# Batch 0's q and k loaded in two parts, w_out ahead of batch 1's v, the last subtile in two column halves: one change to the opening and the tail of an attention + MLP kernel

## The chip, the cores and the metric

One core of a Trainium2 chip. The time is the device time of one execution in microseconds (us). A kernel is run several times beside the kernel before on the same chip, and its median is quoted with the lowest and highest run. A run counts as "slow" when it lies over 1.5% above the fastest of its kernel.

## The reference

Eight batches of causal attention with a decay bias, then a two-layer MLP over all 4608 tokens, in fp32:

```python
scores = scale * q @ k.T                     # 8 batches, 8 heads, 576 tokens, 64 wide
cum    = cumsum(maximum(s, 0))
scores = where(causal, -1e9, scores + minimum(-(cum_i - cum_j), 0))
x      = softmax(scores) @ v                 # -> (4608, 512)
out    = gelu(x @ w_in) @ w_out              # w_in 512 x 2048, w_out 2048 x 512
```

## The kernel before

The tensor engine is kept busy from end to end: the MLP of one chunk of 512 tokens runs with the attention of the next batch woven between its matmuls ("side lists"). Only the opening, where everything waits for loads, and the tail are thin. All loads of q, k, v and the weights are issued by gpsimd. `filler(n)` is n matmuls on zeros: they do no work, they fill a wait. Some words used below: a subtile is 128 tokens. An attend is the product of the softmax weights with v, for which VectorE or gpsimd first scales v (the tile `vv`). PSUM is the memory, divided into banks, that takes the tensor engine's results.

The loads of batch 0's q and k, one per tensor and head group, are 128 runs of 18 tokens (4.5 KB) each, back to back in memory, into 128 partitions:

```python
def qk_runs(src, b, g0, n):                  # LT = 18 tokens per partition
    return bass.AP(tensor=src.tensor, offset=src.offset + (b * H + 4 * g0) * S * D,
                   ap=[[LT * D, 128], [4 * S * D, n], [1, LT * D]])
for g in range(HG):
    for i in range(2):                       # q, k
        load_qk(0, i, g, 1)
```

The opening (cut):

```python
filler(17); cum_sum(); masks(); weights()
nc.scalar.activation(vv[0][:, :, :, D], wb[:, :, 0:H], func=AF.Copy)
filler(3)
filler(3, raws[0, "qk"][:, 1, 0, :128])      # waits for the first k
load_v(0, nc.gpsimd, (0, 1)); load_w(0, 0); load_w(0, 1)       # load_w(0, i): quarter i of w_in
load_v(0, nc.gpsimd, (2, 3)); load_w(0, 2); load_w(0, 3)
scale_v(0, 1, nc.gpsimd)
load_v(0, nc.gpsimd, (4,)); load_qks(1)
load_w(1, 0); load_w(1, 1); load_v(1, nc.gpsimd, (0, 1))       # load_w(1, i): quarter i of w_out
load_w(1, 2); load_w(1, 3); load_v(1, nc.gpsimd, (2, 3, 4))
tr_qk(0, 0, 0); tr_qk(0, 1, 0); sc_first(0, 0)                 # transposes, first scores
# ... the remaining scores, masks, attends and transposes of batch 0
```

The tail. The kernel computes on its way whether its shortcuts hold for the data; a flag is then loaded into a register of each engine, and a branch goes around the general path:

```python
# last subtile: 16 matmuls of 128x512 into one PSUM tile
rv = nc.values_load(bad[0:1, 0:1], min_val=0, max_val=1)
with tc.If(rv > 0):
    ...                                      # general path (not taken here)
y = y_of[LAST[0], sub]
for i, (copy, eng) in enumerate([(nc.vector.tensor_copy, nc.sync), (scalar_copy, nc.scalar)]):
    cols = slice(i * 256, i * 256 + 256)
    copy(o_sb, y[:, cols]); eng.dma_start(out=out[r0 : r0 + 128, cols], in_=o_sb)
```

## Time and profile before

| | kernel before |
|---|---|
| time, median of 3 runs | 315.48 us (315.06 to 315.62) |
| first score / first layer / second layer of chunk 0 starts | 10.23 / 19.46 / 36.74 us |
| first layer of chunk 1 starts | 56.48 us |
| mean granted clock of the tensor engine | 0.999 |

The rows of the table come from the tensor engine's work in order of time, in one profiled run; that run took 315.94 us, 0.4 above the median. The prediction below shows the main lines of the profile. From the page, the clock granted to the tensor engine in 40 slices of 7.85 us (9 is 90% or more) and the count of DMA packets:

```profile
PEclk9999999999999999999999999999999999999999
DMA packets 30979, 36.46 MB, mean 116 GB/s; under 512 B 15648, under 2 KB 20000, under 8 KB 30944
```

And the last matmuls in the timeline (start, duration, what): they end at 305.78 + 3.19 = 308.97, 0.51 us before the first copy at 309.48.

```profile
305.78 3.19 PE L483 MATMUL o_ps<-w_out_r,gT 128*128 128x512 bf16 x14
```

### The profile page before, as it was taken

The numbers are of one execution on the slowest core, as the hardware profiler recorded it, in microseconds if no ns is written. First come the engines' busy times: TensorE is split into PE (matmuls) and PEld (weight loads), VectorE is DVE, ScalarE is ACT, GpSimd is POOL, SyncE is SP. The second block draws the span as 40 slices with busy tenths as digits, with TensorE's granted clock in tenths as the row PEclk, the third lists the DMA queues.
The fourth block names the chain that finished last, engine by engine and source line by source line (L and its number), as shares of the span: only waits on it lengthen the run. The fifth ranks groups of instructions, "written<-read, shape, count | busy, mean of one in ns | idle before, by whom it ended". The sixth has DMA issues, their size and how long they took to land. (4 is left out here: it accounts for less than half of the span.)

```text
span 314.2 us, 6059 instructions
## 1 busy us (share of the span) xinstructions
PE 302.0 (96%) x2475; PEld 155.5 (49%) x2516; DVE 199.0 (63%) x398; ACT 191.0 (61%) x258; POOL 54.5 (17%) x73
## 2 busy tenths in 40 slices
PE   8899999999999999999999999999999999999993
PEld 3477755544554455545454455444544555444441
DVE  7776658599769856975598459955895532250020
ACT  2786878887737673875586658756776666105400
POOL 8653341133001500070007000500000000000000
PEclk9999999999999999999999999999999999999999
DMA  7999999779521973179307951633101331010012
GB/s 124 222 230 209 225 211 270 163 140 211 141 84 25 199 173 102 22 166 206 102 17 171 190 118 36 143 79 91 50 19 42 102 52 26 33 72 32 1 68 75
DMA packets 30979, 36.46 MB, mean 116 GB/s; under 512 B 15648, under 2 KB 20000, under 8 KB 30944
## 3 DMA queue, kind: packets, MB, share of 16 engines
q0 software_dynamic: 11552, 23.07, 38.1%
q1 hardware_dynamic: 19248, 12.80, 14.4%
q8 instruction: 21, 0.34, 0.4%
q14 instruction: 14, 0.11, 0.1%
q10 hardware_dynamic: 144, 0.13, 0.1%
HBM read 36.85 MB, written 9.44 MB: 147 GB/s over the span
## 5 line engine op out<-in xcount | busy, mean ns | idle before, releaser
L483 PE MATMUL o_ps<-w_out_r,gT 128*128 128x512 bf16 x551 | 132.2, 379 | 2.4 <-issue 1.6
L467 PE MATMUL h_ps<-xT,w_in_r 128*128 128x512 bf16 (+1 forms) x625 | 131.4, 357 | 1.3 <-DVE xT L413 0.5
L472 ACT ACTIVATE gT<-h_ps 128x1024 bf16<-128x1024 f32 (+1 forms) x80 | 75.1, 939 | 64.5 <-PE h_ps L467 63.7
L467 PEld LDWEIGHTS <-w_in_r 128*128 128x128 bf16 x640 | 59.8, 98 | 54.2 <-issue 0.6
L483 PEld LDWEIGHTS <-gT 128*128 128x128 bf16 x576 | 51.9, 98 | 56.6 <-issue 3.0
L359 ACT ACTIVATE P<-sc_ps 128x1024 bf16<-128x1024 f32 x56 | 54.3, 1021 | 30.5 <-PE sc_ps L344 30.5
L122 POOL DMA_DIRECT2D raw_v<-in_v_dram x40 | 34.1, 863 | 128.4 <-ACT sq L213 115.7
L493 DVE COPY o_sb<-o_ps 128x512 f32<-128x512 f32 x31 | 21.4, 691 | 46.5 <-PE o_ps L483 46.5
L444 DVE RECIPROCAL rc<-av 128x4 f32<-128x4 f32 (+1 forms) x80 | 14.0, 175 | 39.4 <-PE av L435 39.3
L187 DVE STREAM_TRANSPOSE qkT<-raw_qk 128x576 f32<-128x576 f32 x32 | 37.4, 1242 | 1.8 <-DMA raw_qk<-in_k_dram 1.7
L445 DVE TENSOR_TENSOR x<-av,rc 128x256 bf16<-128x256 f32 (+1 forms) x80 | 33.8, 423 | 3.0
L435 PEld LDWEIGHTS <-P 128*128 128x128 bf16 x576 | 27.1, 97 | 16.5 <-issue 0.8
L205 DVE TENSOR_REDUCE amx<-raw_qk 128x2 f32<-128x2304 bf16 x14 | 35.1, 2532 | 0.0
L435 PE MATMUL av<-vv,P 128*128 128x65 bf16 x576 | 30.5, 193 | 0.6 <-POOL vv L221 0.2
L367 DVE TENSOR_TENSOR P<-P,tri_bf 128x1024 bf16<-128x1024 bf16 (+1 forms) x33 | 22.0, 669 | 9.1 <-ACT P L359 9.1
L221 DVE TENSOR_TENSOR vv<-raw_v,wb 128x512 bf16<-128x512 f32 (+1 forms) x39 | 25.4, 690 | 2.5 <-DMA raw_v<-in_v_dram 2.5
L213 ACT ACTIVATE sq<-raw_v 128x512 bf16<-128x512 f32 (+1 forms) x40 | 24.8, 621 | 0.0
L344 PE MATMUL sc_ps<-qkT 32*128 32x256 bf16 (+2 forms) x560 | 18.2, 250 | 0.0
L344 PEld LDWEIGHTS <-qkT 32*128 32x128 bf16 x560 | 11.7, 92 | 12.4 <-issue 11.6
L498 ACT ACT_TABLE_LOAD x8 | 10.3, 1283 | 0.9 <-PEq L817 0.8
L419 PE MATMUL f_ps<-zero 128*128 128x512 bf16 x26 | 9.3, 494 | 1.2 <-DVE zero L150 1.2
L501 ACT ACT_TABLE_LOAD x8 | 10.3, 1283 | 0.1
(81 smaller groups left out, 92.3 us busy)
## 6 DMA issues: line engine op xcount, KB each, us to landing
out_dram<-o_sb SPq DMA_DIRECT2D x35, 256.0 KB, 2.2
raw_v<-in_v_dram POOLq DMA_DIRECT2D x32, 256.0 KB, 5.5
raw_qk<-in_q_dram POOLq DMA_DIRECT2D x7, 576.0 KB, 7.5
raw_qk<-in_k_dram POOLq DMA_DIRECT2D x7, 576.0 KB, 10.4
w_in_r<-in_moe_w_in_dram POOLq DMA_DIRECT2D x4, 512.0 KB, 12.1
w_out_r<-in_moe_w_out_dram POOLq DMA_DIRECT2D x4, 512.0 KB, 15.8
raw_v<-in_v_dram POOLq DMA_DIRECT2D x8, 128.0 KB, 6.4
raw_qk<-in_q_dram POOLq DMA_DIRECT2D x2, 288.0 KB, 6.2
```

Of the source, the lines that this page charges most:

```text
L122: eng.dma_start(out=t[:n_st, st, :, :], in_=bass.AP(tensor=v.tensor, offset=v.offset + b * H * S * D + st * 128 * D, ap=[[D, n_st], [S * D ...
L187: nc.vector.transpose(qkT[b % 2][:, i, g, :S, :].rearrange("p s e -> p (s e)").bitcast(fp32) .rearrange("p (l j) -> p j l", j=LT), raws[b, ...
L205: nc.vector.tensor_reduce(amx[:, b * HG + g], raws[b, "qk"][:, :, g, :], axis=AX, op=ALU.max, apply_absolute_value=True,)
L213: nc.scalar.activation(sq[:n_st], raws[b, "v"][:n_st, st].rearrange("p h d -> p (h d)"), func=AF.Square, accum_out=sumv[:n_st, b, st : st ...
L221: eng.tensor_tensor(vv[b % 2][:n_st, st, :, 0:D], raws[b, "v"][:n_st, st, :, :], w.unsqueeze(2).to_broadcast([n_st, H, D]), op=MULT,)
L344: nc.tensor.matmul(s_ps[h // 2][:, h % 2, off : off + n], lhsT=qk[r, 1, g, jt * 128 : jt * 128 + 128, e], rhs=qk[r, 0, g, i0 : i0 + n, e], ...
L359: nc.scalar.activation(P[:, 2 * h2 : 2 * h2 + 2, o : o + 512], s_ps[h2], func=AF.Exp, scale=scale)
L435: nc.tensor.matmul(o_ps[:, h, :], lhsT=P[:, h, off : off + 128], rhs=vv[b % 2][:, jt, 4 * g + h, :], start=(i == 0), stop=(i == len(BLK[it ...
L445: nc.vector.tensor_tensor(x_of[b, it][:n, g * 256 : g * 256 + 256].rearrange("p (h d) -> p h d", d=D), o_ps[:n, :, 0:D], rc[:n].unsqueeze( ...
L467: nc.tensor.matmul(h_ps[:, i, :], lhsT=w_in_r[:, ko, ft * 128 : (ft + 1) * 128], rhs=xT[:, ko, c * NB + n0 : c * NB + n1], start=(ko == 0) ...
L472: nc.scalar.activation(gT_of[c][:, f2 * 2 : f2 * 2 + 2, n0:n1], h_ps, func=AF.Gelu)
L483: nc.tensor.matmul(y_of[c, sub], lhsT=gT[:, ft, sub * 128 : (sub + 1) * 128], rhs=w_out_r[:, ft, :], start=(ft == 0), stop=(ft == FT - 1),)
```

## The change

Three things. (1) The opening: q and k of batch 0 come in two parts, tokens 0 to 383 of all heads first, so that scores can start earlier; the order of the opening's work and of gpsimd's loads follows. (2) All of w_out is issued ahead of batch 1's v, and the scalings of v move to later groups of the side lists. (3) The last subtile is computed as two column halves in two PSUM banks, so that the two last copies need not follow one another.

```diff
+    PART = [(0, 384), (384, 576)]
+    def load_part(i, g, part):
+        t0, t1 = PART[part]
+        n = (t1 - t0) // 32 * D
+        src = q if i == 0 else k
+        nc.gpsimd.dma_start(
+            out=raw_qk(0)[:, i, g, t0 * 2 : t1 * 2],
+            in_=bass.AP(tensor=src.tensor, offset=src.offset + 4 * g * S * D + t0 * D,
+                        ap=[[S * D, 4], [n, 32], [1, n]]))
...
-            load_qk(0, i, g, 1)
+            load_part(i, g, 0)
... # after weights():
-    nc.scalar.activation(vv[0][:, :, :, D], wb[:, :, 0:H], func=AF.Copy)
-    filler(3)
-    filler(3, raws[0, "qk"][:, 1, 0, :128])
+    for g in range(HG):
+        for i in range(2):
+            load_part(i, g, 1)
+    filler(1)
+    filler(2, raws[0, "qk"][:, 1, 0, :128])
... # issue order: v0 v1 w0 w1 v2 w2 v3 w3 v4, then
-    load_w(1, 0); load_w(1, 1); load_v(1, (0, 1)); load_w(1, 2); load_w(1, 3); load_v(1, (2, 3, 4))
+    load_w(1, 0..3); load_v(1)
... # batch 1's side lists
-  side[0] = [(sc, b, 0, 0), (scale_v, b, 0), (scale_v, b, 1), (mk, b, 0, 0)]
-  side[5] = [(sc, b, 0, 1), (av, b, 0, 0), (av, b, 0, 1)]
-  side[6] = [(av, b, 1, 0, True), (av, b, 1, 1, True), (scale_v, b, 2), (mk, b, 0, 1)]
-  ...
+  side[0] = [(sc, b, 0, 0), (mk, b, 0, 0)]
+  side[5] = [(sc, b, 0, 1)]
+  side[6] = [(scale_v, b, 0), (scale_v, b, 1), (av, b, 0, 0), (av, b, 0, 1), (mk, b, 0, 1)]
+  side[7] = [(sc, b, 1, 1), (av, b, 1, 0, True), (av, b, 1, 1, True), (gelu_set,)]
+  side[8] = [(scale_v, b, 2), (to_xT, b, 0, True), (av, b, 0, 2), (mk, b, 1, 1)]
+  side[9] = [(to_xT, b, 1, True), (scale_v, b, 3), (av, b, 0, 3)]
... # last subtile
+        for cols in (slice(0, 256), slice(256, 512)):
+            y = yps.tile([128, KO * 128], fp32, tag="mlp", bufs=2, name="o_ps")[:, :256]
+            for ft in range(FT):
+                nc.tensor.matmul(y, lhsT=gT_of[c][:, ft, ...], rhs=w_out_r[:, ft, cols], ...)
```

More of the change, by code (lines that the diff above doesn't have):

```diff
@@ L108, in load_qk, with tr_part @@
         )
+    PART = [(0, 384), (384, 576)]
[5 more added lines that the diff above has]
+            out=raw_qk(0)[:, i, g, t0 * 2 : t1 * 2],
+            in_=bass.AP(
+                tensor=src.tensor, offset=src.offset + 4 * g * S * D + t0 * D,
+                ap=[[S * D, 4], [n, 32], [1, n]],
+            ),
+        )
+    def tr_part(i, g, part):
+        t0, t1 = PART[part]
+        n = (t1 - t0) // 32
+        nc.vector.transpose(
+            qkT[0][:, i, g, t0:t1, :].rearrange("p s e -> p (s e)").bitcast(fp32)
+            .rearrange("p (l j) -> p j l", j=n),
+            raws[0, "qk"][:, i, g, t0 * 2 : t1 * 2].bitcast(fp32).rearrange("p (j w) -> p j w", j=n),
+        )
     def load_qks(b):
@@ L474, in l1_item, with l2_last, l2_item @@
         )
-    def l2_item(c, subs, f0=0, f1=FT, store=True):
+    def l2_last(c, sub):
+        y_of[c, sub] = []
+        for cols in (slice(0, 256), slice(256, 512)):
+            y = yps.tile([128, KO * 128], fp32, tag="mlp", bufs=2, name="o_ps")[:, :256]
+            y_of[c, sub].append((cols, y))
+            for ft in range(FT):
+                nc.tensor.matmul(
+                    y, lhsT=gT_of[c][:, ft, sub * 128 : (sub + 1) * 128], rhs=w_out_r[:, ft, cols],
+                    start=(ft == 0), stop=(ft == FT - 1),
+                )
+    def l2_item(c, subs, f0=0, f1=FT):
         gT = gT_of[c]
@@ L486, in l2_item @@
                 )
-        if f1 == FT and store:
+        if f1 == FT:
             for sub in subs:
@@ L516 @@
     weights()
-    nc.scalar.activation(vv[0][:, :, :, D], wb[:, :, 0:H], func=AF.Copy)
-    filler(3)
-    filler(3, raws[0, "qk"][:, 1, 0, :128])
+    for g in range(HG):
[3 more added lines that the diff above has]
+    filler(2, raws[0, "qk"][:, 1, 0, :128])
     load_v(0, nc.gpsimd, (0, 1))
+    nc.gpsimd.tensor_copy(vv[0][:, :, :, D], wb[:, :, 0:H])
     load_w(0, 0)
     load_w(0, 1)
-    load_v(0, nc.gpsimd, (2, 3))
+    load_v(0, nc.gpsimd, (2,))
+    scale_v(0, 1, nc.gpsimd)
     load_w(0, 2)
+    load_v(0, nc.gpsimd, (3,))
     load_w(0, 3)
-    scale_v(0, 1, nc.gpsimd)
     load_v(0, nc.gpsimd, (4,))
     load_qks(1)
-    load_w(1, 0)
-    load_w(1, 1)
-    load_v(1, nc.gpsimd, (0, 1))
-    load_w(1, 2)
-    load_w(1, 3)
-    load_v(1, nc.gpsimd, (2, 3, 4))
-    tr_qk(0, 0, 0)
-    tr_qk(0, 1, 0)
+    for i in range(4):
+        load_w(1, i)
+    load_v(1, nc.gpsimd)
+    for g in range(HG):
+        for i in range(2):
+            tr_part(i, g, 0)
     sc_first(0, 0)
-    tr_qk(0, 0, 1)
-    tr_qk(0, 1, 1)
-    sc_first(0, 1, (0,))
-    filler(1)
     sc_first(1, 0, (0,))
+    tr_part(0, 0, 1)
+    tr_part(1, 0, 1)
     mk_item(0, 0, 0)
     scale_v(0, 0)
+    filler(1)
     sc_first(1, 0, (1,), 0)
+    filler(1)
+    sc_first(0, 1, (0,), 0)
+    mk_item(0, 1, 0, 0, 2)
     av_item(0, 0, 0)
+    mk_item(0, 1, 0, 2, 4)
+    tr_part(0, 1, 1)
+    tr_part(1, 1, 1)
     av_item(0, 0, 1)
-    mk_item(0, 1, 0, 0, 2)
-    sc_first(0, 1, (1,))
-    mk_item(0, 1, 0, 2, 4)
-    sc_first(1, 1, (0,), 0)
+    sc_first(0, 1, (1,), 0)
     av_item(0, 1, 0)
     av_item(0, 1, 1)
+    sc_first(1, 1, (0,), 0)
+    to_xT(0, 0, True)
     sc_first(1, 1, (1,), 0)
-    to_xT(0, 0, True)
-    filler(1)
     to_xT(0, 1, True)
@@ L621 @@
                 side = [[] for _ in range(16)]
-                side[0] = [(sc, b, 0, 0), (scale_v, b, 0), (scale_v, b, 1), (mk, b, 0, 0)]
+                side[0] = [(sc, b, 0, 0), (mk, b, 0, 0)]
                 side[3] = [(sc, b, 1, 0), (mk, b, 1, 0)]
-                side[5] = [(sc, b, 0, 1), (av, b, 0, 0), (av, b, 0, 1)]
-                side[6] = [(av, b, 1, 0, True), (av, b, 1, 1, True), (scale_v, b, 2), (mk, b, 0, 1)]
-                side[7] = [(to_xT, b, 0, True), (sc, b, 1, 1)]
-                side[8] = [(to_xT, b, 1, True), (scale_v, b, 3), (av, b, 0, 2), (gelu_set,), (mk, b, 1, 1)]
-                side[9] = [(av, b, 0, 3)]
+                side[5] = [(sc, b, 0, 1)]
[3 more added lines that the diff above has]
+                side[9] = [(to_xT, b, 1, True), (scale_v, b, 3), (av, b, 0, 3)]
                 side[11] = [(av, b, 1, 2, True), (scale_v, b, 4), (square_qk, 0, 0), (square_qk, 0, 1)]
@@ L657 @@
             for sub in range(4):
-                l2_item(c, (sub,), store=(c, sub) < LAST)
+                if (c, sub) < LAST:
+                    l2_item(c, (sub,))
+                else:
+                    l2_last(c, sub)
                 if c == B - 1:
@@ L768, in layer_1, with layer_2 @@
                     nc.scalar.activation(g[:, ft, :n], h_ps[:, :n], func=AF.Gelu)
-            def layer_2(h_ps, g, sub):
+            def layer_2(h_ps, g, sub, cols=slice(0, 512)):
                 for ft in range(FT):
                     nc.tensor.matmul(
-                        h_ps, lhsT=g[:, ft, sub * 128 : (sub + 1) * 128], rhs=w_out_r[:, ft, :],
+                        h_ps, lhsT=g[:, ft, sub * 128 : (sub + 1) * 128], rhs=w_out_r[:, ft, cols],
                         start=(ft == 0), stop=(ft == FT - 1),
@@ L789 @@
             for sub in range(LAST[1], 4):
-                layer_2(y_of[LAST[0], sub], g, sub)
+                for cols, y in y_of[LAST[0], sub]:
+                    layer_2(y, g, sub, cols)
     with tc.manual_schedule():
         for sub in range(LAST[1], 4):
-            y = y_of[LAST[0], sub]
             r0 = LAST[0] * NB + sub * 128
-            for i, (copy, eng) in enumerate(
-                [(nc.vector.tensor_copy, nc.sync), (lambda o, a: nc.scalar.activation(o, a, func=AF.Copy), nc.scalar)]
+            for (cols, y), copy, eng in zip(
+                y_of[LAST[0], sub],
+                (nc.vector.tensor_copy, lambda o, a: nc.scalar.activation(o, a, func=AF.Copy)),
+                (nc.sync, nc.scalar),
             ):
-                cols = slice(i * 256, i * 256 + 256)
                 o_sb = ost.tile([128, KO * 128], fp32, tag="osb", bufs=3, name="o_sb")[:, :256]
-                copy(o_sb, y[:, cols])
+                copy(o_sb, y)
                 eng.dma_start(out=out[r0 : r0 + 128, cols], in_=o_sb)
```

## The prediction

> **What bounds the kernel now.** I read the page first (busy shares, slices, DMA row), then what the tensor engine waits for, then its work in order of time for the first 60 us, then the gpsimd engine's in the same stretch (it issues all loads), then each tile's landing times, last the tail.
>
> The page:
> ```profile
> PE 302.0 (96%) x2475; PEld 155.5 (49%) x2516; DVE 199.0 (63%) x398; ACT 191.0 (61%) x258; POOL 54.5 (17%) x73
> DMA  7999999779521973179307951633101331010012
> ```
> The tensor engine is busy from end to end, and nothing in the change removes matmuls that matter, so only the opening and the tail can move. The DMA row (7.85 us a slice) is full through slice 7 and nearly so to slice 10: loads are dense for some 60 us.
>
> The tensor engine's work in time (start us, duration, then what it is):
> ```profile
> 10.23 0.63 PE L389 MATMUL sc_ps<-qkT 32*128 32x256 bf16 x8 [0.47 <-DVE qkT L187]
> ...
> 15.21 0.37 PE L435 MATMUL av<-vv,P 128*128 128x65 bf16 x7 [0.24 <-POOL vv L221]
> 15.51 0.63 PE L389 MATMUL sc_ps<-qkT 32*128 32x256 bf16 x12
> ...
> 19.46 3.65 PE L467 MATMUL h_ps<-xT,w_in_r 128*128 128x256 bf16 x32 [0.52 <-DVE xT L413]
> ...
> 25.88 1.04 PE L467 MATMUL h_ps<-xT,w_in_r 128*128 128x256 bf16 x8
> ...
> 44.57 1.03 PE L483 MATMUL o_ps<-w_out_r,gT 128*128 128x512 bf16 x4
> ```
> First scores at 10.23, first layer at 19.46. At 15.21 the engine waited for a product that gpsimd made. The loads as gpsimd issues them, and the landing times of the two weight tiles (min/median/max):
> ```profile
> 12.14 0.75 POOL L147 DMA_DIRECT2D w_in_r<-in_moe_w_in_dram  x1 [0.77 <-DMA raw_qk<-in_k_dram]
> 14.05 1.10 POOL L221 TENSOR_TENSOR vv<-raw_v,wb 128x512 bf16<-128x512 f32 x1 [1.17 <-DMA raw_v<-in_v_dram]
> ...
> 26.11 1.55 POOL L147 DMA_DIRECT2D w_out_r<-in_moe_w_out_dram  x2 [1.95 <-DMA w_in_r<-in_moe_w_in_dram]
> ```
> ```profile
> DMA to landing us min/median/max: 9.9/12.1/13.7
> ```
> ```profile
> DMA to landing us min/median/max: 14.9/15.8/17.5
> ```
> The last quarter of w_in lands at 12.14 + 13.7 = 25.84, and its first user runs at 25.88. The last quarter of w_out is issued at about 26.88 and lands at 44.4 (+17.5); its first user runs at 44.57. No wait is listed at either place, yet both matmuls follow the landing at once: **the opening is tuned to arrive with its weights.** So I take 25.84 and 44.4 as floors, not coincidences. This is the reading on which the number rests.
>
> The tail:
> ```profile
> 309.48 0.42 DVE L801 COPY o_sb<-o_ps 128x256 f32<-128x256 f32 x1 [3.23 <-DVEq L664]
> 309.94 0.38 ACT L797 ACTIVATE o_sb<-o_ps 128x256 f32<-128x256 f32 x1 [13.72 <-DVE o_sb L801]
> 310.35 0.37 ACTq L802 DMA_DIRECT2D out_dram<-o_sb  x1
> ```
> Two half copies, one after the other: ScalarE waits for VectorE's, as both read one PSUM tile.
>
> **What the Trainium skill says.** "PSUM — Partial Sum Buffer", section "PSUM bank collisions raise a hardware error": two engines may not access one bank in the same partitions at once, readers included, so software orders them. The trace agrees: 309.48 + 0.42, then 309.94. "TensorE: Matmul & The Clock Gate", Part 1: a warm matmul costs N / 2.4 GHz + 2.5 ns from start to start, 109 ns for N = 256 and 216 for 512. The trace agrees: 32 of N = 256 take 3.65 us, less some 0.17 of drain, 109 ns each. "DMA: Bandwidth & Descriptors", section "Why a DMA increments its semaphore by 16 and not by 1": the number of DMA engines k is the largest up to 16 that divides the slowest dimension of both sides, with some gpsimd copies as exceptions. Before, q and k have 128 runs on both sides. The parts have 4 (heads) x 32 at the source, so k may be 4. No load of the trace before has that form, so this stays open.
>
> **The change, part by part.**
>
> *Scores earlier.* The four batch-0 loads were issued at 1.25 to 3.01 and landed, issue plus landing time, at 5.95, 8.9, 10.3 and 11.85. A first part is 2/3 of one. Read off that progress, the four first parts land at about 4.9, 6.9, 8.9 and 9.9; if each runs on 4 engines they go side by side and land at about 7.3, 8.0, 8.5 and 9.1. A transpose of 576 tokens takes 1.24 us, so 384 take about 0.85. The second transpose, which the first score needs, ends near 8 to 9.1. Scores start 1.1 to 2.0 us earlier than 10.23, ScalarE's first exp likewise earlier than 10.90. The transposes become eight instead of four but have the same elements; perhaps 0.2 us more of VectorE, hidden.
>
> *What becomes of that lead.* The second attend item of head group 0 needs vv of subtile 1, which gpsimd makes after v's subtile 1 has landed: 14.05 + 1.10 = 15.15. The same bytes (all q, k, then two subtiles of v) lie ahead of it after the change, so it still comes at about 15.15, and the next score stands behind it on the tensor engine in both kernels. The lead of 1 to 2 us therefore ends at 15.2. What is left is the reordering after it. From 15.5: score 0.57, attend 0.5, score 0.57, transpose 0.25, then the last score, which waits for the sixth exp, near 17.3, then transpose and the 0.42 copy: the first layer starts near 18.9, 0.6 ahead of 19.46. One filler (0.22) and one wait on VectorE are gone from this stretch.
>
> *w_in.* The order is now w0, w1, v2, w2, v3, w3 instead of w0, w1, v2, v3, w2, w3. w2 lands 1 us earlier (22.0 for 23.0), which the earlier start needs. The bytes ahead of w3 do not change, so it lands at 25.8 again. The first layer, 0.6 ahead, gets at most 0.45 ahead at that place (work alone puts it at 25.4) and nothing if w3 comes at 25.84. I expect 0.05 to 0.2 there.
>
> *w_out ahead of v.* It takes 0.52 MB of v, two loads that took about 1.05 us each, from ahead of w2 and w3 of w_out: they land near 39 and 42, no longer a limit. Now v's first two subtiles land last, at the same 44.4. VectorE's scaling takes 0.69 more, so the second attend of group 6 can start at about 45.15. In the tensor engine's time it would come at 45.05 + 0.11 less any lead. So the lead is clipped again: work done by 45.43 before is done by about 45.4 after. The floor moves from one tensor to another; the bytes do not change.
>
> *gpsimd.* A copy of 40 columns moves there from ScalarE (0.38 us there) and waits for the weights (8.5). With eight part loads the first v load waits for the first part to land, and w0 is issued near 9.2 to 10 instead of 6.2, w2 near 15.1 instead of 10.6. The DMA row shows the engines full throughout; bytes outstanding still cover about 2 us, so I expect no hole, but this margin is thin.
>
> *Tail.* 16 matmuls of 512 (15 x 215 + 379 ns = 3.61 us) become 32 of 256 (31 x 109 + 273 = 3.65): +0.04. The two copies then lie in two banks and start together: the later store goes out at about 309.95 instead of 310.35, -0.40. Both copies still wait for the branch around the general path, so the first half cannot be copied under the second. Net -0.36.
>
> **Sum.** -0.36 at the tail, -0.1 to -0.2 at w3, about 0 at 44.4 beyond that, and about -0.15 as an allowance for a DMA stream that gains from part loads side by side. Together -0.65: 315.48 becomes **314.8**.
>
> **Rivals.**
> 1. *The lead survives.* Should the landings at 25.84 and 44.4 be coincidence, or should the stream run faster from the start (between 4 and 6 us it writes at 146 GB/s, later 200 to 270), the lead of 0.6 would stay, more if v's subtile 1 comes earlier too. Total 313.6 to 314.3. For it: no wait for a weight is on the tensor engine's list. Against it: two floors met within 0.2 us.
> 2. *The loads get slower.* Four engines a load, starting one after the other, leave a quarter of them idle until 4 us; runs are shorter, there are four more loads, gpsimd issues later. A shift of w3 passes to the end undiminished: with 1 us, 315.8. Against it: the first loads are slow already, so engine time is not what is short.
> 3. *A stall at batch 1's attend.* v's subtile 1 or its scaling comes 0.5 to 1 us late in group 6. Total 315.3 to 315.8. The dense DMA row speaks for it; against it, w_out leaves the queue earlier by the same amount.
> 4. *A gain over 2%* would need 6.3 us. The tensor engine idles less than that in the whole opening, so I give it nearly nothing.
>
> **Range and chances.** The tail is nearly certain (-0.3 to -0.45). The opening is -1.4 to +0.7, as w3 goes. Eight in ten: 313.8 to 315.7. Faster by over 2%: 0.02; within: 0.97; slower: 0.01.
>
> **What would show each step.** The list of issues: landing times of the parts (side by side means k = 4). Work in time: first score near 8.5 to 9.2; the attend still released by gpsimd's product near 15.15; first layer near 18.9; the w3 matmuls at 25.4 to 25.9, with a wait on the weight tile now or no gain; the attends after group 6 at 44.9 to 45.4, released by VectorE's scaling. Chain of waits: the two last copies together, about 0.4 us less behind them. I am wrong if the first-layer matmuls on w3 start a full microsecond earlier or later than 25.88, or if the attend of 15.2 moves with the scores.

## More of the kernel before

An engine's sequencer is the part that issues its instructions and takes its branches.

The granted clock is the share of full speed that the profile says the tensor engine was given.

## The result, and the profile after

| | before | after |
|---|---|---|
| median (lowest to highest), 4 runs each | 315.55 us (315.06 to 315.70) | 328.69 us (328.16 to 329.02) |
| ratio of fast runs, 95% interval | | 1.0418 (1.0400 to 1.0436) |
| first score starts | 10.23 | 12.11 |
| first layer of chunk 0 starts | 19.46 | 25.38 |
| second layer of chunk 0 starts | 36.74 | 45.17 |
| first layer of chunk 1 starts | 56.48 | 67.06 |
| from last matmul's end to first copy | 0.51 | 2.47 |

A ratio here and below compares the fast runs of the two kernels, so it is not quite the ratio of the medians that are quoted. The change is 4.2% slower; the predicted range ended at 315.7.

The table gives the shape: 8.43 us are lost before the second layer of chunk 0 starts (45.17 - 36.74), 2.15 more by the next chunk's first layer (67.06 - 56.48 = 10.58), and about 2 at the tail.

**Opening, loads.** What the DMA queues did in the first 4 us. In order, before and then after: packets of all queues, then those of the queue that serves gpsimd's loads with the MB they moved and the share of the 16 DMA engines' time that they took, then the loads issued with the median time from issue to landing.

```profile
DMA packets 174, 0.36 MB, mean 91 GB/s; under 512 B 16, under 2 KB 16, under 8 KB 174
q0 software_dynamic: 94, 0.22, 35.9%
raw_qk<-in_k_dram POOLq DMA_DIRECT2D x2, 288.0 KB, 7.9
```
```profile
DMA packets 749, 0.17 MB, mean 42 GB/s; under 512 B 674, under 2 KB 685, under 8 KB 749
q0 software_dynamic: 669, 0.02, 15.6%
raw_qk<-in_k_dram POOLq DMA_DIRECT2D x2, 192.0 KB, 9.4
```

A part has two thirds of the bytes and takes longer to land: 9.4 us for 7.9. In these 4 us the queue handled seven times the packets and moved a tenth of the bytes: nearly all of its packets are tiny (4 bytes each by the trace's packet records). But they do not fill the engines: its packets took 15.6% of the engines' time where they took 35.9% before, and from 4 to 8 us 72.9% for 99.0%. The whole execution shows the tiny packets too. From the page after:

```profile
PEclk9856999999999999999999999999999999999998
DMA packets 34627, 36.48 MB, mean 111 GB/s; under 512 B 18784, under 2 KB 24160, under 8 KB 34592
```

There are 18784 - 15648 = 3136 more packets under 512 B. Four more loads than before are 64 of them: 16 come with each load (the queue of gpsimd's loads has 1056 in the kernel before, for 66 loads). The other 3072 are 3 for each of the 8 x 128 = 1024 runs of the part loads.

**Opening, clock.** The other new thing in this page is the clock row: slices 2 to 4 stand at 8, 5 and 6, where before all stood at 9. By stretches (length, then busy time of the tensor engine, its weight loads, VectorE, ScalarE and gpsimd, granted clock, DMA share, GB/s), before and then after:

```profile
14.00:20.00 6.00, 4.99 (x84) 3.78 (x84) 4.64 (x15) 5.61 (x6) 4.00 (x5) 1.00 1.18 231
20.00:30.00 10.00, 9.70 (x127) 8.67 (x124) 6.68 (x21) 7.50 (x16) 4.90 (x6) 1.00 1.17 212
```
```profile
14.00:20.00 6.00, 6.00 (x52) 3.02 (x53) 3.39 (x9) 3.79 (x4) 3.22 (x5) 0.50 1.17 202
20.00:30.00 10.00, 8.98 (x74) 6.32 (x71) 5.90 (x16) 5.55 (x6) 6.45 (x10) 0.50 1.21 233
```

From 14 to 30 us the tensor engine ran at half clock: "6.00 of 6.00 busy" is 52 matmuls for the 84 of before (not all of the same shapes). The reader who looks only at busy shares would take the after kernel's stretch for the better one. The tensor engine's work in order of time, after, shows what came just ahead:

```profile
11.22 0.61 PE L443 MATMUL f_ps<-zero,raw_qk 128*128 128x512 bf16 x2 [2.74 <-DMA raw_qk<-in_k_dram]
12.11 0.63 PE L413 MATMUL sc_ps<-qkT 32*128 32x256 bf16 x8 [0.28 <-DVE qkT L128]
...
14.10 1.03 PE L413 MATMUL sc_ps<-qkT 32*128 32x256 bf16 x8
...
53.98 0.37 PE L459 MATMUL av<-vv,P 128*128 128x65 bf16 x7 [0.17 <-DVE vv L245]
...
57.90 0.37 PE L459 MATMUL av<-vv,P 128*128 128x65 bf16 x7 [0.39 <-DVE vv L245]
...
60.74 0.37 PE L459 MATMUL av<-vv,P 128*128 128x65 bf16 x7 [1.35 <-DVE vv L245]
```

The first line: the engine stood 2.74 us for the first part of k. Its next score of eight matmuls takes 0.63 us, and the one at 14.10 takes 1.03: the clock fell between them.

**Second layer of chunk 0.** The last three lines above: the attend waits three times for VectorE's scaled v (1.91 us in all). No such waits are listed there before.

**Tail.** The last 32 narrow matmuls, and the copies:

```profile
315.95 3.66 PE L507 MATMUL o_ps<-w_out_r,gT 128*128 128x256 bf16 x32
316.15 0.69 DVE L529 COPY o_sb<-o_ps 128x512 f32<-128x512 f32 x1 [2.76 <-PE o_ps L519]
322.08 0.38 ACT L841 ACTIVATE o_sb<-o_ps 128x256 f32<-128x256 f32 x1 [15.27 <-PEq L707]
322.08 0.42 DVE L845 COPY o_sb<-o_ps 128x256 f32<-128x256 f32 x1 [5.24 <-PEq L707]
```

The copies do start together, as intended, but both are released by the tensor engine's sequencer (PEq) at the line of the branch: 322.08 - (315.95 + 3.66) = 2.47 us after the last matmul ended.

So there are three candidate causes in the opening (slow loads, the fallen clock, the new order), one in the middle and one at the tail. The experiments take them one at a time.

### The profile page after: what moved, and what is told of

The parts are those of the page before. It is cut to its first block, busy times and chain, and to the rows that moved or that the text cites. A ratio compares the mean times of both kernels' runs of the same rounds, so it can differ in the third digit from the quotient of the medians.

```text
span 327.2 us, 6093 instructions
## 1 busy us (share of the span) xinstructions
PE 308.5 (94%) x2487; PEld 160.0 (49%) x2527; DVE 198.7 (61%) x402; ACT 190.9 (58%) x257; POOL 58.5 (18%) x78
## 2 busy tenths in 40 slices
DMA packets 34627, 36.48 MB, mean 111 GB/s; under 512 B 18784, under 2 KB 24160, under 8 KB 34592
## 5 line engine op out<-in xcount | busy, mean ns | idle before, releaser
L491 PE MATMUL h_ps<-xT,w_in_r 128*128 128x512 bf16 (+1 forms) x624 | 134.0, 363 | 1.4 <-DVE xT L437 0.5
L519 PE MATMUL o_ps<-w_out_r,gT 128*128 128x512 bf16 x536 | 129.2, 379 | 2.2 <-issue 1.4
L491 PEld LDWEIGHTS <-w_in_r 128*128 128x128 bf16 x640 | 61.1, 100 | 55.5 <-issue 0.7
L519 PEld LDWEIGHTS <-gT 128*128 128x128 bf16 x560 | 50.3, 98 | 54.7 <-issue 3.0
L383 ACT ACTIVATE P<-sc_ps 128x1024 bf16<-128x1024 f32 x56 | 54.3, 1021 | 30.5 <-PE sc_ps L368 30.5
L459 PE MATMUL av<-vv,P 128*128 128x65 bf16 x576 | 31.4, 195 | 2.8 <-DVE vv L245 2.1
L211 DVE STREAM_TRANSPOSE qkT<-raw_qk 128x576 f32<-128x576 f32 x28 | 32.4, 1239 | 0.0
L421 ACT ACTIVATE P<-sc_ps 128x1024 bf16<-128x1024 f32 x8 | 8.1, 1022 | 8.6 <-PE sc_ps L413 8.6
```

The costliest lines, as they stand in the source:

```text
L211: nc.vector.transpose(qkT[b % 2][:, i, g, :S, :].rearrange("p s e -> p (s e)").bitcast(fp32) .rearrange("p (l j) -> p j l", j=LT), raws[b, ...
L383: nc.scalar.activation(P[:, 2 * h2 : 2 * h2 + 2, o : o + 512], s_ps[h2], func=AF.Exp, scale=scale)
L459: nc.tensor.matmul(o_ps[:, h, :], lhsT=P[:, h, off : off + 128], rhs=vv[b % 2][:, jt, 4 * g + h, :], start=(i == 0), stop=(i == len(BLK[it ...
L491: nc.tensor.matmul(h_ps[:, i, :], lhsT=w_in_r[:, ko, ft * 128 : (ft + 1) * 128], rhs=xT[:, ko, c * NB + n0 : c * NB + n1], start=(ko == 0) ...
L519: nc.tensor.matmul(y_of[c, sub], lhsT=gT[:, ft, sub * 128 : (sub + 1) * 128], rhs=w_out_r[:, ft, :], start=(ft == 0), stop=(ft == FT - 1),)
```

## The experiments

Twelve kernels, all correct against the reference by the comparison used. Some read wrong tokens of batch 0's q and k, which is said where it holds; the comparison passes all the same, so it is no check on these tokens.

### 1. parts_flat: the part loads in another form

The changed kernel, with each part load reading 128 runs of the same length back to back (wrong tokens).

```diff
-    offset=src.offset + 4 * g * S * D + t0 * D,     ap=[[S * D, 4], [n, 32], [1, n]],
+    offset=src.offset + 4 * g * S * D + 4 * t0 * D, ap=[[n, 128], [1, n]],
```

> The changed kernel with its eight part loads of q and k reading 128 evenly spaced runs instead of 4 heads x 32 runs: same number of loads, same run lengths, same bytes, wrong tokens (the result is wrong on purpose). Theory A, the form of the source pattern (its slowest dimension is 4) makes the loads slow and sprinkles them with tiny packets: packets under 512 B fall by about 3070 (three for each of the 1024 runs), the last quarter of w_in lands near 25.8 us instead of 29.6, the clock stays at 1.0, and the time is 318.5 to 320.5 (what is left over before is the stall in the first second-layer pass, about 2.15, and the tail, about 2.35). Rival B, shorter runs and more loads are what is slow: as the changed kernel, 327 to 329.

Measured: 322.29 us (321.61 to 323.59), ratio 1.0223 (1.0188 to 1.0258). From its page:

```profile
PEclk9959999999999999999999999999999999999997
DMA packets 31555, 36.47 MB, mean 114 GB/s; under 512 B 15712, under 2 KB 21088, under 8 KB 31520
```

The 3072 tiny packets are gone (18784 - 15712), with the same number of loads and runs. The parts of k land 5.8 us after issue for 9.4, the queue's share of the engines' time in the first 4 us is 34.9% for 15.6%, and the first score starts at 8.43 instead of 12.11. Theory A holds on the form of the load: 6.4 us come back. The time is some 2 us above its range. A part of that is the clock, which falls here too, later and for a shorter time (number 5 gets 1.0 us back by holding it):

```profile
13.54 0.33 PE L459 MATMUL av<-vv,P 128*128 128x65 bf16 x5 [0.47 <-DVE vv L245]
14.91 0.37 PE L459 MATMUL av<-vv,P 128*128 128x65 bf16 x7 [1.04 <-POOL vv L245]
...
16.47 0.62 PE L459 MATMUL av<-vv,P 128*128 128x65 bf16 x8 [0.39 <-DVE x L469]
17.03 1.03 PE L413 MATMUL sc_ps<-qkT 32*128 32x256 bf16 x12
```

The engine, now early, waits for v in small pieces: 1.90 us in all. By the trace's clock records the clock falls at 16.03, after the first two of these waits (0.47 and 1.04) and at the start of the third; at 16.47 eight attend matmuls take 0.62 instead of 0.41.

### 2. before_4x32: the form alone, put into the kernel before

The kernel before, with whole loads whose source has the form heads x 32 runs. Each run starts 17 tokens after the last instead of 18, so that the two dimensions do not merge into one of 128 (wrong tokens, same sizes and number of loads).

```diff
-            load_qk(0, i, g, 1)                     # ap=[[LT * D, 128], ..., [1, LT * D]]
+            ... ap=[[S * D, 4], [LT * D - D, 32], [1, LT * D]]
```

> The kernel before with its four batch-0 loads of q and k in the 4 x 32 form: still one load each, runs as long as before (4608 bytes read), lanes one token closer so that the two dimensions cannot be merged (wrong result on purpose). Theory A (form): about 384 x 4 = 1540 more packets under 512 B, landings of these loads 2 to 4 us later, first score at 12 to 14 us, and if the tensor engine idles for it, a halved clock behind it; time 318 to 325. Rival B (run length and number of loads): 315.5, no more small packets.

Measured: 325.98 us (325.42 to 327.37), ratio 1.0352 (1.0323 to 1.0381), 1 us above theory A's range. This single line is enough to make a well-running kernel 3.5% slower. From its page and from its tensor engine's work:

```profile
PEclk9856999999999999999999999999999999999999
DMA packets 32515, 36.47 MB, mean 113 GB/s; under 512 B 17184, under 2 KB 21536, under 8 KB 32480
```
```profile
12.41 0.82 PE L426 MATMUL f_ps<-zero,raw_qk 128*128 128x512 bf16 x3 [3.56 <-DMA raw_qk<-in_k_dram]
```

17184 - 15648 = 1536 tiny packets more, which is again 3 for each of 4 x 128 = 512 runs. The four loads land 9.9 to 11.2 us after issue; in the kernel before it was 4.7 to 8.8. The clock row is that of the changed kernel. So the split itself, twice as many loads and shorter runs are not what slows the loads; the form is.

What in the form does it is open. The 4 x 32 loads differ from the flat ones in a second point: their source is not one unbroken block. For the tiny packets this rival is out, as the loads of v and w_in in the kernel before are not unbroken either (8 and 4 runs for each partition) and have just the 16 of every load. For the landing times no run takes the two apart, and it is not the tiny packets' own time that holds the loads, as the 16 engines were on the average less busy and not more.

### 3. tail_alone: the tail's part alone

The kernel before with only the last subtile changed (the last hunk of the diff above).

> The kernel before with the last subtile in two column halves, nothing else. Theory A: the tensor engine's sequencer now reaches the flag load and the branch only when the matmuls end, because 64 instructions of 55 ns each leave it no lead; copies start about 2.4 us after the last matmul instead of 0.5; time +1.5 to +2.4, 317.0 to 317.9. Rival B (the prediction's tail step): copies side by side, -0.36, 315.1.

Measured: 317.88 us (317.58, 317.58, 317.88, 318.44 and 321.28), ratio 1.0083 (1.0062 to 1.0105): +2.36 on the median. The last matmul ends at 312.13 and the copies start at 314.39. The run that was profiled was the one of 321.28: its clock fell from 17 to 24 us, although its opening is that of the kernel before; there the engine had waited 0.91 us for gpsimd's scaled v. Two of the 40 runs of the kernel before that stand beside the experiments point the same way: 317.32 us at a mean clock of 0.989 and 317.76 at 0.985, where the others have 0.994 or more; no trace of these two was kept. **The opening of the kernel before stands near the edge at which the clock falls.**

### 4. bridge: fill the wait for k

The changed kernel with 14 fillers instead of 1 ahead of the wait for the first k part.

```diff
-    filler(1)
+    filler(14)
     filler(2, raws[0, "qk"][:, 1, 0, :128])
```

> The changed kernel with 13 more filler matmuls (about 2.8 us) in the stretch where the tensor engine waited 2.7 us for the first k part. Theory A: the halved clock from 13.7 to 31.7 us is set off by that idle stretch, so with the fillers the clock stays at 1.0; the pass through the first layer is then held by the last quarter of w_in at 29.6 us, 3.7 us later than before instead of 8.4: time 323 to 325. Rival B (the late loads alone cost the time, the clock only follows): no change, 328 to 329, or the clock drops anyway.

Measured: 327.09 us (326.86 to 327.91), ratio 1.0381 (1.0358 to 1.0405). A miss: only 1.6 of the expected 3.7 or more came back. The wait of 2.74 us is filled, and the clock holds until 20 us, but then it falls at 20.29, behind later, smaller waits (0.68, 0.94 and 1.05 us between 13.5 and 19.1):

```profile
17.00:21.00 4.00, 1.85 (x35) 1.49 (x36) 3.81 (x11) 1.81 (x2) 3.01 (x4) 0.91 1.24 216
21.00:24.00 3.00, 3.00 (x37) 2.21 (x35) 1.16 (x4) 1.33 (x3) 2.75 (x5) 0.50 1.18 220
24.00:28.00 4.00, 3.48 (x23) 2.51 (x22) 2.85 (x7) 2.83 (x4) 2.03 (x3) 0.61 1.20 242
```

### 5 and 6. parts_flat_warm, bridge_warm: all the opening's waits filled

parts_flat and bridge, each with 16 more fillers placed in the waits of the first 20 us.

```diff
     sc_first(0, 0)
+    filler(3)
...
+    filler(3)
     av_item(0, 0, 0)
...
+    filler(5)
     av_item(0, 0, 1)
     sc_first(0, 1, (1,), 0)
+    filler(1)
     av_item(0, 1, 0)
+    filler(2)
...
     to_xT(0, 1, True)
+    filler(2)
```

> The evenly spaced part loads again (wrong tokens on purpose), and in addition 16 filler matmuls in the stretches where the tensor engine waited between 10 and 20 us (for v, its scaling and the divisions). Theory A: there the clock had been halved from 16 to 23.6 us because the earlier scores only left a sparser tensor engine behind them; with fillers in the waits it stays at 1.0, and what remains over before is the second-layer pass (about 2.1) and the tail (about 2.35) less a lead of at most 0.5: 319.3 to 320.2. Rival B: the clock falls for another reason: 322 as without fillers.

> The changed kernel with the bridging fillers and the same 16 in the later waits. Theory A: clock 1.0 all through; the slow loads alone remain, and the last quarter of w_in (about 30.6 us against 25.8) sets the first layer: 324 to 325. Rival B: fillers cost more than they save or the clock still falls: 327 or more.

Measured: parts_flat_warm 321.25 us (321.14 to 322.22), ratio 1.018 (1.0138 to 1.0221), a little above the range. bridge_warm 325.28 us (324.96 to 326.45), ratio 1.0309 (1.0266 to 1.0352), just above A's 324 to 325. The clock holds in both, to the last slice (parts_flat_warm, then bridge_warm):

```profile
PEclk9999999999999999999999999999999999999997
PEclk9999999999999999999999999999999999999998
```

Two differences follow. The clock costs 328.69 - 325.28 = 3.4 us in the changed kernel. And with the clock held in both, the form of the loads costs 325.28 - 321.25 = 4.0 us, the fillers being the same but for the 13 ahead of k.

In parts_flat_warm the first layer starts at 19.43, no earlier than before (19.46), though its first scores start 2.0 us earlier (8.21 for 10.23): the lead is gone by then. Numbers 11 and 12 follow that up. (Such times are of one profiled run each. Where the opening is unchanged, in the profiles of before, before_hoist, tail_hoist and tail_narrow, the first layer starts at 18.20 to 19.52 and the second at 36.20 to 36.81.)

### 7. order_alone: w_out's order and the side lists alone

The kernel before with only the second part of the change: w_out ahead of batch 1's v, and the new side lists.

> The kernel before with w_out ahead of batch 1's v and the new side lists, nothing else. Theory A: VectorE's work of groups 6 to 9 (two scalings, attends, masks) now comes in one lump, and the tensor engine waits for scalings: +1.7 to +2.3, 317.2 to 317.8, with waits on the scaled v between 44 and 53 us. Rival B (the prediction's step: the floor only moves): 315.4 to 315.8.

Measured: 317.93 us (317.61 to 318.62), ratio 1.0063 (1.0033 to 1.0093): +2.30 on the median (two of the 11 runs of before beside it were near 317.5, which makes the ratio look smaller than the medians). That is just above theory A's range. The tensor engine and, below it, VectorE in this kernel:

```profile
45.73 0.37 PE L435 MATMUL av<-vv,P 128*128 128x65 bf16 x7 [0.55 <-DVE vv L221]
...
49.64 0.37 PE L435 MATMUL av<-vv,P 128*128 128x65 bf16 x7 [0.39 <-DVE vv L221]
...
52.48 0.37 PE L435 MATMUL av<-vv,P 128*128 128x65 bf16 x7 [1.35 <-DVE vv L221]
```
```profile
44.98 0.69 DVE L221 TENSOR_TENSOR vv<-raw_v,wb 128x512 bf16<-128x512 f32 x1 [0.28 <-DMA raw_v<-in_v_dram]
...
50.61 0.68 DVE L367 TENSOR_TENSOR P<-P,tri_bf 128x1024 bf16<-128x1024 bf16 x1
51.21 0.28 DVE L372 TENSOR_TENSOR P<-P,tri_bf 128x256 bf16<-128x256 bf16 x1
51.41 0.41 DVE L413 COPY xT<-xt_ps 128x512 bf16<-128x512 bf16 x1
51.74 0.68 DVE L221 TENSOR_TENSOR vv<-raw_v,wb 128x512 bf16<-128x512 f32 x1
```

Only the first of the three stalls is a load: v's subtile 1 lands at 44.98 and its scaling follows. At the third, the scaling starts at 51.74 with no idle time and no DMA named: it stands in VectorE's queue behind the masks and a copy. In the kernel before the scaling of the same subtile started at 49.42. The whole pass of chunk 0's second layer takes 22.27 us (36.53 to 58.80) against 19.74 (36.74 to 56.48): +2.5. No run takes w_out's order and the side lists apart; by this trace 0.55 of the 2.29 us of stalls is the load and the rest VectorE's order.

### 8. tail_hoist: the flag loaded earlier

tail_alone, with the load of the branch's flag moved ahead of the last subtile.

```diff
+                if (c, sub) == LAST:
+                    rv = nc.values_load(bad[0:1, 0:1], min_val=0, max_val=1)
...
-    rv = nc.values_load(bad[0:1, 0:1], min_val=0, max_val=1)
```

> The two column halves at the tail on the kernel before, with the flag's load into the registers moved ahead of the last subtile (before it was after it). Theory A: it is the load that takes the 2 us; ahead of the matmuls it is hidden, the two copies start within 0.6 us of the last matmul: 314.9 to 315.3. Rival B: the branch itself or the fetch of the code behind it takes the time: 316.5 to 317.9.

Measured: 317.27 us (317.16 to 318.34), ratio 1.0055 (1.0023 to 1.0087). The gap from the last matmul to the copies is 1.83 us (308.47 to 310.30) for 2.26, which is rival B: the load is some 0.4 to 0.6 of it, and what else lies in the rest, the branch or the fetch of the code behind it, was not taken apart.

### 9. before_hoist: the same in the kernel before

> The kernel before, with the load of the branch's flag moved ahead of the last subtile and nothing else. Its last subtile keeps 16 matmuls of 512[...], and only 0.52 us lay between the last matmul's end and the first copy. Theory A (the flag's load lies under the matmuls already, as the sequencer is some us ahead): nothing to gain, 315.3 to 315.8. Theory B (part of those 0.52 us is the load): up to 0.4 less, 315.1 to 315.3. In no case slower by more than 0.3.

Measured: 315.30 us (314.65 to 315.97), ratio 0.9987 (0.9961 to 1.0012), beside 315.50 for before. No gain that can be told from none: theory A. It was also the only candidate for a version that beats both kernels, and it does not show that it does.

### 10. tail_narrow: narrow matmuls, one bank

The kernel before with the last subtile as 32 matmuls of 256 columns into one PSUM tile, the copies as before.

```diff
+        halves = [slice(0, 512)] if store else [slice(0, 256), slice(256, 512)]
+        for cols in halves:
-                    y_of[c, sub], lhsT=..., rhs=w_out_r[:, ft, :],
+                        y_of[c, sub][:, cols], lhsT=..., rhs=w_out_r[:, ft, cols],
```

> The kernel before, with the last subtile as two column halves of 16 matmuls each in ONE bank (one tile); both copies wait as before, one after the other. Theory A (32 matmuls of 109 ns with 32 weight loads, about 55 ns for each instruction, leave the tensor engine's sequencer no lead, so the flag's load and the branch come after the last matmul): the gap from the last matmul's end to the first copy is 2.2 to 2.5 us as with the whole tail change, and as the copies are serial again the time is 317.6 to 318.4. Theory B (the two banks, or the copies that start together, cause the gap): the gap stays at 0.5 and the time is 315.3 to 315.9.

Measured: 318.29 us (317.92 to 320.50), ratio 1.0103 (1.0063 to 1.0144): theory A. The last matmul ends at 299.80 + 9.27 = 309.07 and the copy starts 2.23 us later:

```profile
299.80 9.27 PE L485 MATMUL o_ps<-w_out_r,gT 128*128 128x512 bf16 x58
...
311.30 0.42 DVE L803 COPY o_sb<-o_ps 128x256 f32<-128x256 f32 x1 [5.00 <-PEq L666]
311.76 0.34 SPq L804 DMA_DIRECT2D out_dram<-o_sb  x1
311.76 0.38 ACT L799 ACTIVATE o_sb<-o_ps 128x256 f32<-128x256 f32 x1 [15.49 <-DVE o_sb L803]
```

So neither the two banks nor the simultaneous copies make the gap; cutting the matmuls does. The worth of the two banks is seen in the trace: the copies are one after the other here, 0.46 us apart (311.30, 311.76). The medians differ by as much, 318.29 against 317.88, but that is within the spread of the runs.

The traces hold one thing more, the fetches of instructions. A fetch of 16 KB starts 2.43 us before the last matmul ends in the kernel before (306.54), and 0.22, 0.20 and 0.24 us before it in tail_narrow, tail_alone and the changed kernel (308.85, 311.93, 319.37); with the flag loaded early (tail_hoist, 307.56) it is 0.91. The first copy comes 2.45 to 2.94 us after the start of this fetch in these five (in before_hoist, where it starts 2.99 us ahead of the end, 3.71 us after). So with narrow matmuls the way to the branch is reached some 2.2 us later against the matmuls. That the copies wait for this fetch is not shown.

### 11 and 12. parts_only_flat_warm, parts_only_flat_lean: the split with its costs taken out

parts_flat_warm with the order of w_out, the side lists and the tail of the kernel before, so that only the split opening is left, with well-formed loads (wrong tokens) and the clock held. Number 12 then drops the 5 fillers that stand behind v's subtile 1.

> The split opening alone: part loads that read 128 evenly spaced runs (wrong tokens, on purpose), fillers in the waits so that the tensor clock holds, and the order of w_out, the batch-1 side lists and the tail of the kernel before. It is the change with its three costs taken out. Theory A (the prediction's step: the lead of the earlier scores ends at v's subtile 1 and at the last quarter of w_in, so the split is worth nothing): first layer within 0.3 us of the 19.46 of before, time 315.0 to 316.0. Theory B (there is a gain that the other parts hid): under 314.8. If the costs don't add up, over 316.3, another cost is left in the opening.

> parts_only_flat_warm without its last three groups of fillers (5 matmuls, 1.1 us of tensor work that came after v's subtile 1 and ahead of the first layer); the fillers ahead of it stay, so the clock should hold (1.0 to 20 us; if a half-clock stretch shows, the run says nothing of this point). In parts_only_flat_warm v's scaled subtile 1 was ready at 14.74 and the first layer still started at 19.49. Theory A (the fillers themselves took the lead behind that point, and behind it a floor of the loads takes what is regained): the first layer starts at 18.3 to 19.0, PE then shows waits for VectorE or a DMA before 31 us, the second layer starts within 0.3 of the 36.74 of before, and the time is 315.3 to 316.5. Theory B (the lead is worth something once the fillers are gone): second layer under 36.3 and time under 315.1. Theory C (the chain exp, mask, attend, transpose, and not the fillers, set 19.49): first layer at 19.3 to 19.6 again, time 316.2 to 317.

Measured: 316.72 us (315.87 to 318.26), ratio 1.0040 (1.0001 to 1.0079), and 316.72 us (316.25 to 317.23), ratio 1.0042 (1.0021 to 1.0062). Both are over theory A's ranges and show no gain, so another cost is left in the opening (number 12's time lies in theory C's range, its first layer, 19.05, between A's and C's). In number 12 the tensor engine's work shows where the lead of the early scores (8.08 for 10.23) goes:

```profile
19.05 3.65 PE L491 MATMUL h_ps<-xT,w_in_r 128*128 128x256 bf16 x32 [0.52 <-DVE xT L437]
...
24.78 0.41 PE L459 MATMUL av<-vv,P 128*128 128x65 bf16 x8 [0.72 <-DVE x L469]
```
```profile
23.48 0.69 DVE L245 TENSOR_TENSOR vv<-raw_v,wb 128x512 bf16<-128x512 f32 x1 [1.75 <-DMA raw_v<-in_v_dram]
```

The first layer is 0.41 early (19.05 for 19.46), which is within the spread of unchanged openings. At 24.78 it is 0.48 late (24.30 before), because VectorE waited for v's subtile 3 until 23.48 and only then came to the divisions that free the attend's PSUM. In the new issue order that subtile stands behind w2 of w_in. The 0.5 then stays to the second layer (37.23 for 36.74), to chunk 1 (56.95 for 56.48) and to the first of the last copies (309.97 for 309.48). The second layer starts at 37.12 to 37.23 in all three kernels with well-formed parts and a held clock, later than any of the unchanged openings. Of the remaining 0.6 of the 1.14 us, some 0.4 is that the profiled run of the kernel before (315.94 us) was slower than its median; the two profiled runs differ by 0.83, and the last 0.3 of that lies behind the last copies.

### The sum

Each cost as a difference of medians, each against what ran beside it or against its partner:

| part | from | us |
|---|---|---|
| narrow last matmuls | tail_alone - before: 317.88 - 315.52 | +2.36 |
| w_out's order and side lists | order_alone - before: 317.93 - 315.63 | +2.30 |
| the split and its order, well-formed, clock held | parts_only_flat_lean - before: 316.72 - 315.58 | +1.14 |
| form of the part loads | bridge_warm - parts_flat_warm: 325.28 - 321.25 | +4.03 |
| fallen clock | after - bridge_warm: 328.69 - 325.28 | +3.41 |
| sum | | +13.24 |
| measured | 328.69 - 315.55 | +13.14 |

The first three were measured apart, in kernels of their own; together they are 5.80, and the kernel that has all three, parts_flat_warm (with five more fillers than number 12), measured 321.25 - 315.63 = 5.62. The last two rows are differences along a chain of kernels; that they bring the sum home to 0.1 is partly built in. The clock's row is what fillers could save, and fillers are not free.

## Why the prediction was wrong, point by point

**Scores earlier (wrong; the step that failed first).** The prediction had the first parts land at 4.9 to 9.9 us and scores 1.1 to 2.0 us earlier. The parts landed at 9.8 to 13.0, and the scores started 1.88 later (12.11). The form "4 heads x 32" was seen and left open, and both its readings assumed an early landing ("side by side and land at about 7.3, 8.0, 8.5 and 9.1"). Each run of that form brings three extra tiny packets and the loads land some 9 us after issue. With another form of the same loads (parts_flat) scores start at 8.43, so the estimate of the bytes was right and that of the form was not. With the clock held, the form costs 4.0 us. Rival 2, "the loads get slower", was the right rival, sized at 1 us and dismissed because "engine time is not what is short". Engine time was indeed not short (15.6% in the first 4 us for 35.9%), and the loads were late all the same: the inference failed, and what holds them inside the form is open. The prediction's own sign of being wrong came true: the matmuls on w3 start at 34.31, not at 25.88.

**What the prediction did not have at all: the clock.** It took matmul durations as constants. The clock halved at 13.5, after the wait at 8.5 to 11.2, and stayed so to 30.5; filling that wait and the later ones brings 3.4 us back. Nothing in the prediction asks what an idle tensor engine does to the work after it.

**What becomes of the lead (right that it ends, wrong that a gain is left).** "The lead of 1 to 2 us therefore ends at 15.2": in parts_flat the attend behind v's subtile 1 waits 1.04 us for gpsimd's product and starts at 14.91, near the 15.15 that was named. With well-formed loads and the clock held, the second layer is not early (37.17 and 37.23 for 36.74). "The first layer starts near 18.9": 19.05 in parts_only_flat_lean, which the spread of unchanged openings (18.20 to 19.52) does not let count as a hit. What is left of the split is a cost of 1.14 us where the sum had a gain of some 0.3. The changed kernel never had the lead.

**w_in (reasoning right, floor not the one that bit).** Quarter w3 as a floor at 25.8 did not bite in number 12 (no wait for w_in is listed there), because the same reordering had put v's subtile 3 behind w2 and made that the floor, at 23.48. The prediction counted only bytes ahead of w3. In tail_hoist, whose opening is that of before and a little earlier, a wait of 0.23 us for a quarter of w_in at 25.33 shows that the floor is real.

**w_out ahead of v ("about 0": wrong, +2.30).** (Where the prediction writes here that v leaves from ahead of w2 and w3 "of w_in", w_out is meant.) The landing was judged nearly right: v's subtile 1 at 44.98 for 44.4, and the attend at 45.73 for 45.15. What failed is the sentence "VectorE's scaling takes 0.69 more": it counted one scaling by its duration, not where all the moved scalings stand in VectorE's order. Two later ones, behind masks, divisions and a copy, held the attends for 0.39 and 1.35 us. Rival 3, a stall there, was sized at 0.5 to 1 us.

**gpsimd ("no hole"): wrong for the changed kernel, though not by its issue order.** The page's DMA row reads 5999999647 in its first ten slices for 7999999779. With well-formed parts and the same order of the opening's loads it reads 7999999679 and 7999999779 (parts_only_flat_lean, parts_only_flat_warm). So the thin first slice comes with the form of the loads.

**Tail (mechanism half right, size and sign wrong: -0.36 predicted, +2.36 measured).** Matmuls in 3.66 us for the predicted 3.65, copies side by side, worth some 0.4: all as said. And "both copies still wait for the branch" was said, but used only to deny a further gain. The question not asked was when the branch is done. Before, its cost lay under 16 wide matmuls. After, 32 matmuls and 32 weight loads pass in 3.66 us, 57 ns for each instruction, and the copies behind the same flag load and branch start 2.47 us after the last matmul. Cutting the matmuls is shown to be enough (tail_narrow); that the sequencer has no lead over instructions so short is the reading that fits it and the times of the instruction fetches, not one that a run shows by itself.

## What to carry to other kernels

Before splitting a load, look at the form in which it is issued and not only at its bytes, and count its packets under 512 B; a form of 4 x 32 runs that does not merge made loads of the same bytes land 2.4 to 5.2 us later. Look at the granted clock whenever a change may let the tensor engine wait, even in pieces of half a microsecond to one, for a busy share of 100% can hide half speed. And work that stands behind another engine's queue or under the last wide matmuls has a position, not just a duration: moving or thinning what covers it lays it bare.

## What the Trainium skill lacked or had wrong

- "DMA: Bandwidth & Descriptors", section "Why a DMA increments its semaphore by 16 and not by 1", gives the rule that the largest k up to 16 which divides the slowest dimension of both sides is used. By that rule the form 4 x 32 against 128 partitions would have k = 4; no view here names the engines. The page advises, in "Rules for kernel authors", against an outermost dimension under 16. It lacks what the form costs a load issued by gpsimd: 3 extra packets under 512 B for each run (3072 for 1024 runs, 1536 for 512; none with 128 evenly spaced runs), and 9.9 to 11.2 us from issue to landing for 4.7 to 8.8. If k = 4, twelve other engines with a quarter as many tiny packets as there are runs would give just that number (12 x 32 = 384 for 128 runs); this is worked out from the rule, not seen.
- "TensorE: Matmul & The Clock Gate", Part 1, has the clock fall after at least one idle window of about 3.4 us, and return after about 3.4 us of busy time; its section "A second HAM failure mode: psum-queue depth-cycling" adds that frequent short idle times can do it too, without saying how many or how long. Here it fell after waits of 0.47 and 1.04 us between 13.07 and 14.91 us (parts_flat, at 16.03) and after one of 2.74 us (the changed kernel, at 13.48), and it stayed at 0.50 while the tensor engine was busy for 6.00 of 6.00 us (14 to 20 us), until about 30. Stretches of half clock lasted 6.83 us (parts_flat, bridge, tail_alone) or 17.07 us (the changed kernel, before_4x32), which is two and five times 3.41. What ends one is open. The page's two values of the clock agree with the traces (1.00 and 0.50).
- "Advanced Engine Details and Errata", section "Control Flow Timing", gives about 108 ns for a compare-and-branch. With the flag's load taken out ahead (tail_hoist), 1.83 us still lie between the last matmul and the copies that the branch releases. "Runtime: NRT & Kernel Launch", section "Instruction fetch mechanics", says that a taken branch out of the fetched window stalls for a fetch, which would fit a branch around a large block. The traces show a 16 KB fetch just there (number 10), but not that the copies wait for it.
- No page says that splitting the last matmuls before a branch in two exposes that branch: 2.23 us for 0.51 (tail_narrow).
